# An H3 convolution and a linear-attention block on one core: 3,712 added matmuls in small array tiles, behind the denominators and at the end

## The chip, the cores and the metric

The kernel runs on one core of one Trainium2 chip. Its engines are TensorE (PE, with PEld for its weight loads), VectorE (DVE), ScalarE (ACT), GpSimd (POOL) and SyncE (SP, which issues the DMAs). The metric is the device time of one execution in microseconds (us).

## What is computed

Two independent blocks on sequences of S = 2048 rows and D = 576 columns in bf16, whose outputs stand side by side in a result of 1 x 2048 x 1152.

```
A:  k_shift = sum over t<4 of k shifted by t rows, times shift_k
    kv = k_shift * v
    y  = irfft(rfft(kv, 2S) * rfft(ssm_k, 2S))[:S] + kv * ssm_D     # a causal convolution
    a  = q * y
B:  q, k, v = x @ wqkv, 32 heads of 18
    phi(t) = where(t > 0, t + 1, exp(t)) + 1e-6
    kv = phi(k)^T v ;  z = sum over s of phi(k)
    b  = ((phi(q) kv) / (phi(q) z + 1e-6)) @ wo
result = concat(a, b)
```

## The kernel before

Block A is a long convolution written as matmuls with DFT matrices. The D = 576 channels are cut into five chunks (`ACH`: four of 128, one of 64). For each chunk the filter (`h`) and the input (`u`) go through the same stages. `h_T` transposes the filter on TensorE. `s1` (line 460) multiplies with the DFT matrix `K.G`, eight 128x128x128 matmuls for one PSUM tile. `tr` (line 467) is a DMA transpose of the evicted tile `Ch` or `Cu` into `Cth` or `Ctu`; these share two buffers. `s2` (line 483) does eight matmuls with 64 contraction rows, 32 output columns and 512 moving columns, in eight different array tiles. `prod` multiplies filter and input on DVE, `i1` (line 507) and `i2` (lines 520 and 521) transform back, and DVE multiplies by q. The shift convolution `conv` runs on DVE and POOL.

Block B makes `pqT` = phi(q) transposed (`b_q`, line 406) and `pk` = phi(k) (`b_k`, line 397). `b_G` (line 570) forms x^T phi(k), `b_kv` (583, 590) the per-head products and sums, and `b_M` (601) folds `wo` in. `b_den` makes the denominators: twenty matmuls of 512 columns (line 610) and twenty of one column (line 614), each with 32 output columns, go to four column tiles of `den_ps`; then DVE adds and takes the reciprocal `rden` (lines 617 to 621). `b_bc` (line 635) spreads `rden` over the heads and scales `pqT`, and `b_out` (line 644) multiplies with `M`, evicts on ACT (649) and stores by DMA (650).

The order of the work is written out by hand: `ORDER` is a string of units, such as `den`, `o.3` (rows 3 of `b_out`) or `h2.2.1.1.A` (stage `s2` of the filter, chunk 2, half 1, x = 1, evicted by ACT). Each unit issues its instructions to all engines as it is reached, and each engine runs its own instructions in that order. All matmul results go to one PSUM pool of four buffers, named `psum` (line 257), with the one tag `big`; each buffer is two banks of 512 float32. A unit that asks for a tile gets the buffer that was taken four requests before, and its first matmul waits until that one's readers are through.

Around the first place of the change the order is `i2.0.1 h2.2.0.0.A h2.2.1.0.A den h2.2.1.1.A i1.1.1.0.A lwo M.0 ... ut.2.0 u2.2.0.0.A M.2 ut.2.1 bc.3.0`. At the end it is `o.2 i2.4.0 st.2 o.8 o.10`. The kernel already has a unit that issues matmuls whose result is not read: `wu.40` (`_warm`, line 64), forty of 128x128 with 128 columns on a tile of zeros, near the start. `K.F[0]`, which the change reads, is one of the two transposed DFT matrices, 128 x 2048 in bf16, made by `f_T` near the start and read by `i2` until the end.

Of the kernel before, what the change touches and what calls it, by code (L numbers as in the profile page):

```python
# [8 lines left out]
FP32 = mybir.dt.float32  # L9
# [19 lines left out]

ORDER = """  # L30
wm io wu.0 ix.0 sin.1 id ix.1 hl.0 iw wk wu.40 sin.0 hT.0.D FT.1.D h1.0.0.0.A h1.0.1.0.A FT.0.D h1.0.1.1.A
h1.0.0.1.A iv sw W lw.0 xd.2 q.2.0 hc lw.1 k.8 q.2.2 q.2.1 ls Wj hl.1 hT.1.D k.9 k.11 k.10 h1.1.1.0.D xd.0 k.3
kl.0 cv.0.0.D one h1.1.0.0.A k.1 ht.0.0 h2.0.0.0.A h2.0.0.1.A eps cv.0.1.DD cv.0.2.DD q.0.1 h1.1.1.1.A q.0.0
h1.1.0.1.A xd.3 q.3.0 q.0.2 vl.0 cv.0.3.PDD k.2 cv.1.0.P k.0 ht.0.1 h2.0.1.1.A q.3.1 k.12 u1.0.1.1.A k.15
h2.0.1.0.D ht.1.1 h2.1.1.0.A k.13 u1.0.0.1.A hl.2 hT.2.D u1.0.0.0.A cv.1.1.PD k.14 xd.1 u1.0.1.0.A xl.2
cv.1.2.DD cv.1.3.DPP ht.1.0 xl.1 h2.1.1.1.A q.1.1 h2.1.0.1.A h2.1.0.0.A q.1.0 q.1.2 h1.2.1.0.A ut.0.1 k.7
u2.0.1.0.D u2.0.1.1.A k.6 h1.2.0.1.A k.4 ut.0.0 u2.0.0.1.D u2.0.0.0.A k.5 pX.0.0 pT.0.0 u1.1.1.0.A u1.1.1.1.A
q.3.2 u1.1.0.1.A xl.0 xl.3 kl.1 pX.0.1 pT.0.1 u1.1.0.0.A es G.0 vl.1 h1.2.0.0.A h1.2.1.1.A cv.2.0.D cv.2.1.DD
cv.2.2.DD G.2 ut.1.0 G.4 u2.1.0.1.D u2.1.0.0.A ut.1.1 i1.0.0.1.A hl.3 i1.0.0.0.A i1.0.1.1.A i1.0.1.0.A
cv.2.3.DDD ql.0 cv.3.0.D cv.3.1.DD u2.1.1.1.A ht.2.0 u2.1.1.0.A pX.1.1 pT.1.1 hT.3.A G.1 lwv pX.1.0 pT.1.0  # L40
h2.2.0.1.A ht.2.1 G.3 cv.3.2.DD u1.2.0.0.A i2.0.0 kl.2 u1.2.1.1.A u1.2.1.0.A kv u1.2.0.1.A i2.0.1 h2.2.0.0.A
h2.2.1.0.A den h2.2.1.1.A i1.1.1.0.A lwo M.0 i1.1.0.1.A i1.1.0.0.A i1.1.1.1.D ut.2.0 u2.2.0.0.A M.2 ut.2.1
bc.3.0 u2.2.0.1.A bc.0.1 h1.3.0.1.A bc.4.0 h1.3.0.0.A bc.0.0 h1.3.1.1.A vl.2 h1.3.1.0.A hl.4 ht.3.0 i2.1.1 M.1
u2.2.1.1.A cv.3.3.PPP bc.2.0 M.4 i2.1.0 cv.4.0.P M.3 u2.2.1.0.A bc.1.0 u1.3.0.0.A ht.3.1 hT.4.D u1.3.1.0.A
u1.3.1.1.D pX.2.1 u1.3.0.1.A cv.4.1.PP o.3 ql.1 pX.2.0 pT.2.0 pT.2.1 h2.3.0.1.A h2.3.0.0.A ut.3.0 o.0 o.7 bc.2.1
h2.3.1.1.A h2.3.1.0.A i1.2.0.0.D cv.4.2.PP cv.4.3.DDP i1.2.0.1.A i1.2.1.0.A i1.2.1.1.A ut.3.1 bc.1.1 bc.3.1 o.5
i2.2.0 u2.3.0.0.A u2.3.0.1.A i2.2.1 u1.4.1.1.A o.6 u1.4.1.0.D u1.4.0.0.A bc.4.1 u1.4.0.1.A ut.4.0 h1.4.1.1.A o.1
u2.3.1.0.D u2.3.1.1.A pX.3.1 h1.4.0.1.A o.11 h1.4.0.0.A h1.4.1.0.D ht.4.0 o.14 o.9 pT.3.1 pX.3.0 pT.3.0
u2.4.0.1.A u2.4.0.0.D ql.2 i1.3.1.0.A i1.3.1.1.A i1.3.0.1.D st.0 i1.3.0.0.A h2.4.0.0.D h2.4.0.1.A pX.4.0 o.15
i2.3.1 o.12 pT.4.0 i2.3.0 st.1 o.4 i1.4.0.1.D i1.4.0.0.A o.13 i2.4.1 o.2 i2.4.0 st.2 o.8 o.10  # L50
"""


# [12 lines left out]
def _warm(tc, psum, K, n):  # L66

    nc = tc.nc
    zero = K.sm[:, 1984:2048].bitcast(BF)
    if n:  # L70
        ps = psum.tile([128, 128], FP32, name="warm_ps", tag="big")
        for _ in range(n):
            nc.tensor.matmul(ps[:], lhsT=zero, rhs=zero, start=True, stop=True)
    else:
        nc.vector.memset(zero, 0.0)


def _head_consts(tc, cpool, K):
# [153 lines left out]
def kernel(  # L232
# [13 lines left out]
    nc = tc.nc  # L246
# [3 lines left out]
    q = A_q[0]  # L250
    k = A_k[0]
# [5 lines left out]
    psum = ctx.enter_context(tc.tile_pool(name="psum", bufs=4, space=PSUM))  # L257
# [33 lines left out]
    big = ctx.enter_context(tc.tile_pool(name="big", bufs=1, side="right"))  # L291
# [24 lines left out]
    K = Consts()  # L316
# [16 lines left out]
    Wj = lpool.tile([128, 4, D], BF, name="Wj")  # L333
# [42 lines left out]
    st = {}  # L376
# [24 lines left out]
    def b_q(g, pair):  # L401
        ps = psum.tile([128, 2, 512], FP32, name="q_ps", tag="big")
        for j, c in enumerate(pair):
            h0, hn = HCH[c]
            for t in range(5):
                nc.tensor.matmul(ps[0:hn, j, :], lhsT=wqk[:, t, h0:h0 + hn], rhs=xT[g][:, t, :],  # L406
                                 start=(t == 0), stop=(t == 4))
        n = len(pair)
        hn = HCH[pair[0]][1]
        phi(ps[0:hn, 0:n, :], pqT[0:hn, pair[0]:pair[0] + n, g * 512:(g + 1) * 512], hn)  # L410
# [253 lines left out]
    def pair(g, n):  # L664
        b_q(g, ((0, 1), (2, 3), (4,))[n])

    UNITS = {
        'xl': load_x, 'one': ones, 'wm': one_w, 'lw': load_w, 'ls': load_shift, 'Wj': shift_w, 'eps': eps_col,
        'id': lambda: _ident(tc, cpool, K), 'io': lambda: _small(tc, cpool, slotx, K),
# [16 lines left out]
        'pX': lambda ci, f: prod(ci, f, 'X'),  # L686
        'i1': i1, 'i2': i2, 'st': store_A,
        'k': b_k, 'q': pair, 'lwv': load_wv, 'lwo': load_wo, 'G': b_G, 'kv': b_kv, 'M': b_M,
        'den': b_den, 'es': b_esel, 'wu': lambda n: _warm(tc, psum, K, n), 'bc': b_bc, 'o': b_out,
    }  # L690
    with tc.manual_schedule():
        for unit in ORDER.split():
            name, *arg = unit.split('.')
            UNITS[name](*[int(c) if c.isdigit() else c for c in arg if c])

# [29 lines left out]
```

## Time and profile before

| | |
|---|---|
| median of 2 runs (170.94 to 171.16) | 171.05 us |
| span of the profiled execution | 170.0 us |
| the median less this span: what lies around it | 1.05 us |
| instructions | 4,984 |
| matmuls, and as many weight loads | 2,176 |
| DMA packets, bytes | 81,704, 32.58 MB |
| mean granted TensorE clock over the span | 0.995 |

The page gives the busy time of each engine, the chain of work that ended last, and the costliest groups of instructions. A row of a group names line, engine, operation, the tiles it writes and reads, the weights' rows*columns, the moving operand's shape and the count; then busy time in us, the mean of one in ns, and the idle time ahead with what ended it. In the timeline a row begins with start and length, in the chain too; in the view by stretches the columns are PE, PEld, DVE, ACT and POOL busy time with counts, then the granted clock, the DMA engines' share, and GB/s. A matmul's mean is from its start to its modelled end; consecutive ones overlap, so that their rate is higher than one by that mean.

### The profile page before, as it was taken

How to read it: one execution, taken by the hardware profiler on the slowest of the kernel's cores; microseconds unless marked ns; L12 is line 12 of the kernel's file. 1: busy time of each engine (PE TensorE's matmuls, PEld its weight loads, DVE VectorE, ACT ScalarE, POOL GpSimd, SP SyncE). 2: the span in 40 equal slices, each digit the busy share in tenths (PEclk: the TensorE clock that was granted, in tenths of full speed). 3: DMA queues.
4: the chain of work that ended last, by engine and by line, in shares of the span. 5: the costliest groups of instructions: out<-in, count | busy, mean ns of one | idle time of the engine just before them, and what ended most of it. 6: DMA issues, size and time to landing. Idle time of an engine off the chain costs nothing.

```text
span 170.0 us, 4984 instructions
## 1 busy us (share of the span) xinstructions
PE 159.0 (94%) x2176; PEld 106.9 (63%) x2176; DVE 139.7 (82%) x159; ACT 122.8 (72%) x142; POOL 70.9 (42%) x76
## 2 busy tenths in 40 slices
PE   4779999999999799999999999999999999999990
PEld 4768566665575456565685586857856765677750
DVE  7995589998989867999599887997999777999530
ACT  3458987977788899923597477989897778784431
POOL 7998982027693397000000049999900400000000
PEclk9999999999999999999999999999999999999997
DMA  5999699799989999999998655980959957988685
GB/s 147 273 268 250 119 267 136 137 272 225 145 183 217 263 178 318 290 213 219 306 214 196 106 150 40 182 159 18 146 126 276 202 128 69 237 180 258 191 244 117
DMA packets 81704, 32.58 MB, mean 192 GB/s; under 512 B 57432, under 2 KB 80978, under 8 KB 81682
## 3 DMA queue, kind: packets, MB, share of 16 engines
q1 hardware_dynamic: 81682, 32.26, 91.0%
q8 instruction: 17, 0.28, 0.7%
q14 instruction: 5, 0.04, 0.1%
HBM read 15.48 MB, written 4.72 MB: 119 GB/s over the span
## 4 chain that ended last, share of the span: by engine, by line
PE 77%; DMA 11%; DVE 6%; ACT 3%; issue 0%; ACTq 0%
PE q_ps L406 12%; PE g_ps L570 12%; PE k_ps L397 11%; PE o_ps L644 10%; PE s_ps L460 8%; PE i_ps L507 8%; DMA Ctu<-Cu 7%; PE s_ps L483 5%; DMA Cth<-Ch 4%; PE hT_ps L443 2%; PE i_ps L520 2%; PE i_ps L521 2%; PE bc_ps L635 1%; PE kv_ps L583 1%; DVE mp L138 1%; DVE mp L139 1%
## 5 line engine op out<-in xcount | busy, mean ns | idle before, releaser
L429 POOL TENSOR_TENSOR at<-k,Wj 128x2048 bf16<-128x2048 bf16 (+1 forms) x5 | 16.4, 3289 | 36.3 <-DVE at L430 36.2
L406 PE MATMUL q_ps<-xT,wqk 128*126 128x512 bf16 (+1 forms) x100 | 23.3, 381 | 0.0
L644 PE MATMUL o_ps<-wo_M,pqT 126*128 126x512 bf16 (+3 forms) x160 | 21.9, 286 | 0.0
L397 PE MATMUL k_ps<-wqk,xT 128*128 128x512 bf16 (+1 forms) x160 | 21.8, 286 | 0.0
L460 PEld LDWEIGHTS <-G 128*128 128x128 bf16 x320 | 17.6, 98 | 5.2 <-issue 2.1
L570 PE MATMUL g_ps<-pk,x_sb 128*128 128x512 bf16 (+3 forms) x160 | 20.4, 286 | 0.0
L277 ACT ACTIVATE Cu<-s_ps 128x1024 bf16<-128x1024 f32 (+1 forms) x18 | 16.6, 951 | 2.8 <-PE s_ps L460 2.4
L397 PEld LDWEIGHTS <-xT 128*128 128x128 bf16 x160 | 11.4, 98 | 11.1 <-issue 1.1
L644 PEld LDWEIGHTS <-pqT 126*128 126x128 bf16 (+1 forms) x160 | 11.2, 97 | 10.7 <-issue 0.8
L406 PEld LDWEIGHTS <-wqk 128*126 128x126 bf16 (+1 forms) x100 | 12.5, 131 | 8.2 <-issue 1.2
L277 ACT ACTIVATE Ch<-s_ps 128x1024 bf16<-128x1024 f32 (+1 forms) x18 | 16.3, 952 | 1.4 <-PE s_ps L460 0.8
L507 PE MATMUL i_ps<-W,T 64*128 64x128 bf16 x288 | 16.6, 216 | 0.4 <-DVE pqT L638 0.4
L649 ACT ACTIVATE ob<-o_ps 128x576 bf16<-128x576 f32 x16 | 10.4, 653 | 8.9 <-PE o_ps L644 8.7
L570 PEld LDWEIGHTS <-x_sb 128*128 128x128 bf16 (+1 forms) x160 | 10.8, 101 | 9.5 <-issue 0.2
L507 PE MATMUL i_ps<-W,X 64*128 64x128 bf16 x288 | 16.5, 216 | 0.0
L277 ACT ACTIVATE T<-s_ps 128x1024 bf16<-128x1024 f32 x16 | 15.8, 1021 | 0.6 <-PE s_ps L483 0.6
L277 ACT ACTIVATE V<-i_ps 128x1024 bf16<-128x1024 f32 x14 | 13.6, 1027 | 2.8 <-PE i_ps L507 2.1
L390 DVE SCALAR_TENSOR_TENSOR pqT<-pqT,q_ps 126x1024 bf16<-126x1024 bf16 (+1 forms) x12 | 12.2, 1037 | 3.8 <-ACT pqT L389 3.8
L522 DVE TENSOR_TENSOR q<-i_ps,q 128x1024 bf16<-128x1024 f32 (+1 forms) x10 | 11.2, 1116 | 4.6 <-PE i_ps L521 4.6
L389 ACT ACTIVATE pqT<-q_ps,neg 126x1024 bf16<-126x1024 f32 (+1 forms) x12 | 11.6, 968 | 4.3 <-PE q_ps L406 4.3
L430 POOL TENSOR_TENSOR at<-at 128x2048 bf16<-128x2048 bf16 (+1 forms) x4 | 12.4, 3094 | 5.4 <-DVE at L429 5.2
L433 POOL TENSOR_TENSOR v<-at,v 128x2048 bf16<-128x2048 bf16 (+1 forms) x3 | 10.3, 3419 | 9.8 <-DVE at L430 9.6
(120 smaller groups left out, 335.4 us busy)
## 6 DMA issues: line engine op xcount, KB each, us to landing
x_sb<-in_B_x_dram SPq DMA_DIRECT2D x4, 576.0 KB
out_dram<-ob SPq DMA_DIRECT2D x16, 144.0 KB, 4.0
h_sb<-in_A_ssm_k_dram SPq DMA_DIRECT2D x4, 512.0 KB
k<-in_A_k_dram SPq DMA_DIRECT2D x2, 1024.0 KB, 9.1
v<-in_A_v_dram SPq DMA_DIRECT2D x2, 1024.0 KB, 6.6
q<-in_A_q_dram SPq DMA_DIRECT2D x2, 1024.0 KB
out_dram<-q SPq DMA_DIRECT2D x2, 1024.0 KB
wqk<-in_B_wqkv_dram SPq DMA_DIRECT2D x2, 576.0 KB
```

The costliest lines, as they stand in the source:

```text
L277: nc.scalar.activation(out=out, in_=in_, func=ACT.Copy)
L389: nc.scalar.activation(out=out_ap, in_=ps_ap, func=ACT.Exp, bias=K.neg1[0:n, :])
L390: nc.vector.scalar_tensor_tensor(out=out_ap, in0=out_ap, scalar=1.0, in1=ps_ap, op0=ALU.min, op1=ALU.max)
L397: nc.tensor.matmul(ps[:, n0:n1], lhsT=xT[r // 4][:, t, rr * 128:(rr + 1) * 128], rhs=wqk[:, t, D + n0:D + n1], start=(t == 0), stop=(t == 4))
L406: nc.tensor.matmul(ps[0:hn, j, :], lhsT=wqk[:, t, h0:h0 + hn], rhs=xT[g][:, t, :], start=(t == 0), stop=(t == 4))
L429: on[0].tensor_tensor(out=t_, in0=kk[:, 3 - stage:19 - stage], in1=wb(stage), op=ALU.mult)
L430: on[1].tensor_tensor(out=a_, in0=a_, in1=t_, op=ALU.add)
L460: nc.tensor.matmul(ps[:, bi, 0:dc], lhsT=K.G[ri][:, b, :], rhs=xf(b), start=True, stop=True)
L507: nc.tensor.matmul(ps[:, r, g, :], lhsT=s[key, hf][64 * r:64 * r + 64, z, x, 128 * g:128 * g + 128], rhs=K.W[64 * r:64 * r + 64, m, :], st ...
L522: nc.vector.tensor_tensor(out=qs, in0=ps[:, :, 0:dc], in1=qs, op=ALU.mult)
L570: nc.tensor.matmul(ps[0:fn, n0:n1], lhsT=x_sb[:, r, f0:f0 + fn], rhs=pk[:, r, n0:n1], start=(r == 0), stop=(r == 15))
L644: nc.tensor.matmul(ps[:, n0:n1], lhsT=pqT[0:hn, c, r * 128:(r + 1) * 128], rhs=B['M'][0:hn, c, n0:n1], start=(c == 0), stop=(c == 4))
```

## The change

A function `_tiles` issues matmuls of given kinds, and a unit `pb` calls it: `pb.1` stands in `ORDER` right behind `den`, `pb.2` at the very end. Beside these two words the string is only broken into lines in another way. No unit is moved or removed, and nothing reads what the added matmuls write.

A kind is (kr, mc, n, count, step, mix): kr contraction rows, mc weight columns, n moving columns, `count` matmuls, each with its own weight load. They go round all 128/kr x 128/mc tiles of the array, the row tile changing fastest, and each row tile writes its own PSUM bank. The weights are columns of `K.F[0]`, shifted by one from matmul to matmul; with step 16 they are sixteen columns apart. With mix, one matmul of the full array with 512 columns follows every sixteen. `pb.1` has two kinds, 512 + 256 = 768 matmuls; `pb.2` has eleven, 2,944, with 32 more full ones from the mix.

```diff
+def _tiles(tc, psum, zero, kinds):
+    nc = tc.nc
+    for kind in kinds:
+        kr, mc, n, count, step, mix = kind
+        nr, ncol = 128 // kr, 128 // mc
+        ps = [psum.tile([128, 2, 512], FP32, name="tiles_ps", tag="big") for _ in range((nr + 1) // 2 + mix)]
+        for i in range(count):
+            r, c = i % nr, i // nr % ncol
+            rows = zero[kr * r:kr * r + kr]
+            nc.tensor.matmul(ps[r // 2][mc * c:mc * c + mc, r % 2, 0:n],
+                             lhsT=rows[:, i % 64:i % 64 + mc * step].rearrange("p (a s) -> p a s", s=step)[:, :, 0],
+                             rhs=rows[:, 0:n], start=True, stop=True)
+            if mix and i % 16 == 15:
+                nc.tensor.matmul(ps[-1][:, 0, :], lhsT=zero[:, 0:128], rhs=zero[:, 0:512], start=True, stop=True)
...
+    def tiles(part):
+        zero = K.F[0][:].rearrange("p b k -> p (b k)")
+        if part == 1:
+            _tiles(tc, psum, zero, ((64, 32, 64, 512, 1, 0), (64, 64, 64, 256, 1, 0)))
+        else:
+            _tiles(tc, psum, zero, ((64, 32, 64, 512, 1, 0), (64, 32, 64, 256, 16, 0), (64, 64, 64, 512, 1, 0),
+                                    (64, 64, 32, 256, 1, 0), (32, 64, 64, 256, 1, 0), (32, 32, 64, 256, 1, 0),
+                                    (128, 128, 128, 64, 1, 0), (128, 64, 64, 128, 1, 0), (128, 64, 128, 64, 1, 0),
+                                    (64, 64, 64, 512, 1, 1), (64, 128, 128, 128, 1, 0)))
...
-h2.2.1.0.A den h2.2.1.1.A i1.1.1.0.A lwo M.0 i1.1.0.1.A i1.1.0.0.A i1.1.1.1.D ut.2.0 u2.2.0.0.A M.2 ut.2.1
+u1.2.1.1.A u1.2.1.0.A kv u1.2.0.1.A i2.0.1 h2.2.0.0.A h2.2.1.0.A den pb.1 h2.2.1.1.A i1.1.1.0.A lwo M.0 i1.1.0.1.A
...
-i2.3.1 o.12 pT.4.0 i2.3.0 st.1 o.4 i1.4.0.1.D i1.4.0.0.A o.13 i2.4.1 o.2 i2.4.0 st.2 o.8 o.10
+o.2 i2.4.0 st.2 o.8 o.10 pb.2
...
-        'den': b_den, 'es': b_esel, 'wu': lambda n: _warm(tc, psum, K, n), 'bc': b_bc, 'o': b_out,
+        'den': b_den, 'es': b_esel, 'wu': lambda n: _warm(tc, psum, K, n), 'pb': tiles, 'bc': b_bc, 'o': b_out,
```

More of the change, by code (lines that the diff above doesn't have):

```diff
@@ L31 @@
 wm io wu.0 ix.0 sin.1 id ix.1 hl.0 iw wk wu.40 sin.0 hT.0.D FT.1.D h1.0.0.0.A h1.0.1.0.A FT.0.D h1.0.1.1.A
[L32 to L40, printed above, removed]
@@ L41 @@
-h2.2.0.1.A ht.2.1 G.3 cv.3.2.DD u1.2.0.0.A i2.0.0 kl.2 u1.2.1.1.A u1.2.1.0.A kv u1.2.0.1.A i2.0.1 h2.2.0.0.A
-h2.2.1.0.A den h2.2.1.1.A i1.1.1.0.A lwo M.0 i1.1.0.1.A i1.1.0.0.A i1.1.1.1.D ut.2.0 u2.2.0.0.A M.2 ut.2.1
-bc.3.0 u2.2.0.1.A bc.0.1 h1.3.0.1.A bc.4.0 h1.3.0.0.A bc.0.0 h1.3.1.1.A vl.2 h1.3.1.0.A hl.4 ht.3.0 i2.1.1 M.1
-u2.2.1.1.A cv.3.3.PPP bc.2.0 M.4 i2.1.0 cv.4.0.P M.3 u2.2.1.0.A bc.1.0 u1.3.0.0.A ht.3.1 hT.4.D u1.3.1.0.A
-u1.3.1.1.D pX.2.1 u1.3.0.1.A cv.4.1.PP o.3 ql.1 pX.2.0 pT.2.0 pT.2.1 h2.3.0.1.A h2.3.0.0.A ut.3.0 o.0 o.7 bc.2.1
@@ L46 @@
[L46 to L49, printed above, removed]
-i2.3.1 o.12 pT.4.0 i2.3.0 st.1 o.4 i1.4.0.1.D i1.4.0.0.A o.13 i2.4.1 o.2 i2.4.0 st.2 o.8 o.10
+h1.0.0.1.A iv sw W lw.0 xd.2 q.2.0 hc lw.1 k.8 q.2.2 q.2.1 ls Wj hl.1 hT.1.D k.9 k.11 k.10 h1.1.1.0.D xd.0 k.3 kl.0
@@ new lines @@
+cv.0.0.D one h1.1.0.0.A k.1 ht.0.0 h2.0.0.0.A h2.0.0.1.A eps cv.0.1.DD cv.0.2.DD q.0.1 h1.1.1.1.A q.0.0 h1.1.0.1.A
+xd.3 q.3.0 q.0.2 vl.0 cv.0.3.PDD k.2 cv.1.0.P k.0 ht.0.1 h2.0.1.1.A q.3.1 k.12 u1.0.1.1.A k.15 h2.0.1.0.D ht.1.1
+h2.1.1.0.A k.13 u1.0.0.1.A hl.2 hT.2.D u1.0.0.0.A cv.1.1.PD k.14 xd.1 u1.0.1.0.A xl.2 cv.1.2.DD cv.1.3.DPP ht.1.0
+xl.1 h2.1.1.1.A q.1.1 h2.1.0.1.A h2.1.0.0.A q.1.0 q.1.2 h1.2.1.0.A ut.0.1 k.7 u2.0.1.0.D u2.0.1.1.A k.6 h1.2.0.1.A
+k.4 ut.0.0 u2.0.0.1.D u2.0.0.0.A k.5 pX.0.0 pT.0.0 u1.1.1.0.A u1.1.1.1.A q.3.2 u1.1.0.1.A xl.0 xl.3 kl.1 pX.0.1
@@ new lines @@
+pT.0.1 u1.1.0.0.A es G.0 vl.1 h1.2.0.0.A h1.2.1.1.A cv.2.0.D cv.2.1.DD cv.2.2.DD G.2 ut.1.0 G.4 u2.1.0.1.D
+u2.1.0.0.A ut.1.1 i1.0.0.1.A hl.3 i1.0.0.0.A i1.0.1.1.A i1.0.1.0.A cv.2.3.DDD ql.0 cv.3.0.D cv.3.1.DD u2.1.1.1.A
+ht.2.0 u2.1.1.0.A pX.1.1 pT.1.1 hT.3.A G.1 lwv pX.1.0 pT.1.0 h2.2.0.1.A ht.2.1 G.3 cv.3.2.DD u1.2.0.0.A i2.0.0 kl.2
+u1.2.1.1.A u1.2.1.0.A kv u1.2.0.1.A i2.0.1 h2.2.0.0.A h2.2.1.0.A den pb.1 h2.2.1.1.A i1.1.1.0.A lwo M.0 i1.1.0.1.A
+i1.1.0.0.A i1.1.1.1.D ut.2.0 u2.2.0.0.A M.2 ut.2.1 bc.3.0 u2.2.0.1.A bc.0.1 h1.3.0.1.A bc.4.0 h1.3.0.0.A bc.0.0
@@ new lines @@
+h1.3.1.1.A vl.2 h1.3.1.0.A hl.4 ht.3.0 i2.1.1 M.1 u2.2.1.1.A cv.3.3.PPP bc.2.0 M.4 i2.1.0 cv.4.0.P M.3 u2.2.1.0.A
+bc.1.0 u1.3.0.0.A ht.3.1 hT.4.D u1.3.1.0.A u1.3.1.1.D pX.2.1 u1.3.0.1.A cv.4.1.PP o.3 ql.1 pX.2.0 pT.2.0 pT.2.1
+h2.3.0.1.A h2.3.0.0.A ut.3.0 o.0 o.7 bc.2.1 h2.3.1.1.A h2.3.1.0.A i1.2.0.0.D cv.4.2.PP cv.4.3.DDP i1.2.0.1.A
+i1.2.1.0.A i1.2.1.1.A ut.3.1 bc.1.1 bc.3.1 o.5 i2.2.0 u2.3.0.0.A u2.3.0.1.A i2.2.1 u1.4.1.1.A o.6 u1.4.1.0.D
+u1.4.0.0.A bc.4.1 u1.4.0.1.A ut.4.0 h1.4.1.1.A o.1 u2.3.1.0.D u2.3.1.1.A pX.3.1 h1.4.0.1.A o.11 h1.4.0.0.A
@@ L51 @@
+h1.4.1.0.D ht.4.0 o.14 o.9 pT.3.1 pX.3.0 pT.3.0 u2.4.0.1.A u2.4.0.0.D ql.2 i1.3.1.0.A i1.3.1.1.A i1.3.0.1.D st.0
+i1.3.0.0.A h2.4.0.0.D h2.4.0.1.A pX.4.0 o.15 i2.3.1 o.12 pT.4.0 i2.3.0 st.1 o.4 i1.4.0.1.D i1.4.0.0.A o.13 i2.4.1
+o.2 i2.4.0 st.2 o.8 o.10 pb.2
 """
```

## The prediction

> **What bounds the kernel now.** First the page's shares and its chain that ended last:
>
> ```profile
> PE 159.0 (94%) x2176; PEld 106.9 (63%) x2176; DVE 139.7 (82%) x159; ACT 122.8 (72%) x142; POOL 70.9 (42%) x76
> PE 77%; DMA 11%; DVE 6%; ACT 3%; issue 0%; ACTq 0%
> ```
>
> TensorE (PE) is busy for 94% of the span and carries 77% of the chain. What is put into its queue in the middle therefore moves nearly everything after it. Next the chain in order of time, at the two places of the change (start, length, what):
>
> ```profile
> 105.38 0.11 PE den_ps L614 x19
> 105.49 0.34 PE s_ps L483 x8
> 105.83 1.00 PE i_ps L507 x32
> ...
> 163.28 2.48 PE o_ps L644 x20
> 165.76 0.02 issue
> 165.78 0.65 ACT ob L649
> ```
>
> The first addition stands between 105.49 and the eight s_ps matmuls; there PE goes on without a gap. The second stands behind the last o_ps matmul at 165.76. The stretches around them:
>
> ```profile
> 106.00:112.00 6.00, 5.93 (x150) 4.54 (x145) 5.84 (x4) 5.71 (x7) 5.92 (x2) 1.00 0.89 168
> 112.00:120.00 8.00, 7.24 (x94) 5.17 (x92) 6.74 (x7) 7.10 (x10) 7.77 (x5) 1.00 0.45 91
> 165.80:170.00 4.20, 0.00 (x0) 0.00 (x0) 0.00 (x0) 0.64 (x1) 0.00 (x0) 0.79 0.52 117
> ```
>
> PE works 5.93 of 6 us behind the first place, and not at all in the last 4.2 us: only there is cover, 170.0 - 165.76 = 4.24 us, while the last eviction and output DMA finish.
>
> **What a small matmul costs.** A row's mean is a latency; the rate is read from how many fit into a time. From the groups by shape, the timeline and the chain:
>
> ```profile
> L483 PE MATMUL s_ps<-Cth,W 64*32 64x512 bf16 x144 | 6.1, 383 | 0.9 <-DMA Cth<-Ch 0.9
> 105.42 0.41 PE L483 MATMUL s_ps<-Cth,W 64*32 64x512 bf16 x8
> 83.09 0.56 PE s_ps L483 x16
> 83.65 3.68 PE i_ps L507 x128
> 14.52 0.89 PE s_ps L460 x16
> 101.85 0.36 PE z_ps L590 x5
> ```
>
> Eight 64x32 matmuls in eight different tiles end 0.41 us after the first began, though one takes 0.383: seven steps in 0.027 us, 3.9 ns each, weight load included. I call such a set a round. Sixteen take 0.56 us on the chain and eight 0.34, so one more round of 512 columns is 0.22 us, and 0.12 us of the 0.34 is the change to another tile form. At 128 columns a full-array matmul steps by 0.89/16 = 56 ns, and i_ps L507, in two 64-row tiles, by 3.68/64 = 57.5 ns per round of two. With one column, den_ps L614 takes 0.11 us for nearly five rounds of four: 25 ns. The line through 220 and 56 ns gives 29 ns for a round of 64 columns; for 32 columns I take the 25.
>
> The other half is supply: can instructions arrive at one pair (weight load and matmul) every 3.6 ns for longer than one burst? The page shows how the program is loaded:
>
> ```profile
> q8 instruction: 17, 0.28, 0.7%
> ```
>
> 2,176 + 2,176 PE instructions in 17 packets is 256 each: 128 pairs a packet. 0.7% of 16 engines' 170.0 us is 19.0 us, 1.12 us a packet, or 8.75 ns a pair if one packet follows another. Bounds of the supply: 3.9 ns (the burst above, 16 instructions long) and 28.75 ns (i_ps L507: 128 pairs in 3.68 us, the fastest stretch as long as a packet). I take 8.75, nearest to the row that measures the loading itself, with one packet already there at the start (the L507 stretch uses up a packet without a gap).
>
> **Part 1, 768 pairs behind the denominators.** By the array: 512 in eight tiles are 64 rounds, 64 x 29 = 1.86 us; 256 in four tiles of 64x64 are 64 rounds, 1.86 us; two more changes of form, 0.24: 3.96 us. By the supply: 128 pairs at 3.6 ns (0.46) and 640 at 8.75 (5.60), with 0.24: 6.30 us, which I take. At 28.75 ns it is 22.3.
>
> Nothing covers it: the rows show PE without a gap there. DVE's reciprocal runs beside it and will end earlier relative to PE, but PE has other work before the first bc_ps anyway. The later PE idles, 0.42 and 0.31 us, might be filled:
>
> ```profile
> 114.80 0.61 PE L460 MATMUL s_ps<-hT,G 128*128 128x128 bf16 x8 [0.42 <-ACT Ch L277]
> 115.71 0.61 PE L460 MATMUL s_ps<-hT,G 128*128 128x128 bf16 x8 [0.31 <-ACT Ch L277]
> 107.48 6.13 DMA Ctu<-Cu
> 104.02 6.10 SPq L467 DMA_TRANSPOSE Ctu<-Cu  x2
> ```
>
> They hang on the landing of Ctu. The second transpose (ut.2.1) reuses the buffer that h2.2.1.1 reads, which is the unit right behind the added matmuls. So SP's queue waits longer too (its v and h loads behind it as well), and I let this idle move along: gain 0, at best 0.73. The two PSUM buffers that part 1 takes were last read by i2.0.1 (DVE) and h2.2.0.0 (ACT). A late reader there would cost at most one eviction, 1.02 us; I take 0:
>
> ```profile
> 103.60 1.23 DVE L522 TENSOR_TENSOR q<-i_ps,q 128x1024 bf16<-128x1024 f32 x1 [0.35 <-PE i_ps L521]
> 103.97 2.95 ACT L277 ACTIVATE T<-s_ps 128x1024 bf16<-128x1024 f32 x3 [0.24 <-PE s_ps L483]
> ```
>
> DVE is through at 104.83 and ACT's first of three before 105.49.
>
> **Part 2, 2,944 pairs and 32 full ones at the end.** By the array, in the order of the code: 512 in 64x32 1.86; 256 of the same with weights 16 columns apart 0.93; 512 in 64x64 (128 rounds) 3.71; 256 in 64x64 of 32 columns (64 rounds at 24 to 25 ns) 1.54; 256 in 32x64 0.93; 256 in 32x32, 3.3 to 3.9 ns each, 0.85. These 2,048 pairs make 9.82 us. Then 64 full ones at 56 ns 3.56; 128 in 128x64 1.86; 64 in 128x64 of 128 columns 1.79; 128 in 64x128 as in L507 3.68. The mixed kind: sixteen small ones are four rounds and a change of form (0.23 us), and a lone 512-column matmul between two forms is 0.34 less the burst, 0.32; 32 x 0.55 = 17.6. Ten changes of form at 0.12 are 1.2. Sum by the array: 39.5 us.
>
> Unknown prices: weights of 64 columns. The five L590 matmuls load up to 126 columns for 7 moving ones, 72 ns each, so 64 columns are at most 36 ns against 29; under the supply rate a round of four takes 35 anyway: 0. Spaced weights: transposing h_sb loads its columns 16 apart too (sixteen in 1.15 us below), 72 ns against 56, so at most 0.5 us over 32 rounds; these have a quarter of the columns, and I take 0.
>
> ```profile
> 87.88 1.15 PE hT_ps L443 x16
> ```
>
> By the supply the first 2,048 take 0.46 + 1,920 x 8.75 ns (16.8) = 17.3 us in place of 9.8; the kinds behind them need a pair only every 14 ns or more, and stay. 17.3 + 28.5 + 1.2 = 47.0. At 28.75 ns it is 90.4. The 4.24 us behind 165.76 now lie beside this; closing after the last matmul I estimate at 0.3 (its latency is 0.2 to 0.4 in the rows): net 47.0 - 3.94 = 43.1.
>
> **Sum.** The profiled execution has a span of 170.0 us; the median of the runs is 171.05, so 1.05 lies around it and stays. 171.05 + 6.3 + 43.1 = 220.4 us.
>
> The Trainium skill's page "Runtime: NRT & Kernel Launch", section "Instruction fetch mechanics", says that PE holds 2,048 instructions, refilled in blocks of 256, and that crossing a block is mostly hidden. The trace agrees on the block (256 a packet); how many are held no run here shows. By that rule the sum is the array's, the first rival.
>
> **The rivals.** Array alone: if several packets are loaded ahead, 1,536 instructions of part 1 are all there, and the refill at 1.12 us a packet keeps up with part 2. For it: L507 used up a packet, and PE stood still for none. Against: nothing in the trace ever drew more than 256 instructions in 3.68 us. 171.05 + 3.96 + 39.5 - 3.94 = 210.6 us.
>
> Loading without overlap: if a packet is only asked for when the last one is begun, and the asking takes as long as the transfer, 2.24 us for 128 pairs, 17.5 ns each. Part 1 11.9, part 2 34.1 + 28.9 + 1.2 = 64.1: 243.1 us. At the bound of 28.75 ns, 279.8.
>
> A halved clock: PE can run slower than the granted-clock column says.
>
> ```profile
> L73 PE MATMUL warm_ps<-sm 128*128 128x128 bf16 x40 | 4.4, 313 | 2.4 <-DVE sm L75 2.4
> ```
>
> These 40 at the start take 110 ns each, twice the 56 of later ones. If many small tiles count as little activity, rounds double: 7.9 and 79 us, 254 us. Against: no row in the middle shows it. The page "TensorE: Matmul & The Clock Gate" of the Trainium skill, Part 1, describes such a gate, half rate until the array has been busy; the L73 row agrees, and whether small tiles count as busy no row shows.
>
> Not slower: matmuls whose result nobody reads might be dropped when the kernel is built; then the time stays 171. L73 speaks against it: 40 such matmuls are in the trace. Hiding cannot do it: at 3.9 ns a pair 2,976 pairs are 11.6 us, and only 4.24 + 3.4 (2%) are free at the end; it would decide from 2.6 ns.
>
> **How the numbers follow.** Forecast 0.42, array alone 0.25, loading without overlap 0.18, halved clock 0.10, bound of the supply 0.03, not slower 0.02. The likeliest gives 220.4. From 206 (array alone, less 0.73 and some of the mixed kind) to 250 lie the first three, 0.85; the halved clock is left out. A measurement of this kernel tells about 2% from no change: faster 0.01, same 0.01, slower 0.98.
>
> **What would show it.** In the profile after: some 29 more instruction packets on q8 (7,488 instructions); about 6 us of small matmuls behind L614, and the eight s_ps that much later; in part 2 the 64x32 kind in 4 to 5 us (1.9 for the array alone, 9 without overlap), and each mixed group of 17 in 0.55 us. The 128x128 kind at 56 ns shows the clock. I am wrong if the first kinds step by rounds of 29 ns, or stop at every 128 pairs for over a microsecond.

## The result, and the profile after

The changed kernel takes 281.45 us (280.45 to 282.45, 2 runs) against 171.05: 1.645 times as long, 95% interval 1.630 to 1.659. The forecast was 220.4 us with a range to 250. That it gets much slower was right; the size was not. Where two runs of one kernel lie over 1.5% apart, the longer one at a lower clock, only the shorter is used; of the experiments this concerns `lumps192`. From `_tiles` on the line numbers of the kernel after are 17 higher: L500 is the L483 of before, L524 the L507, and L88 and L92 are the added matmuls. The page of the kernel after, its shares, its code packets and the costliest group:

```profile
PE 226.2 (81%) x5920; PEld 162.0 (58%) x5920; DVE 139.6 (50%) x159; ACT 122.8 (44%) x142; POOL 70.8 (25%) x76
PEclk9989999999999999555999999997555555559999
...
q8 instruction: 46, 0.75, 1.2%
...
PE 73%; issue 17%; DVE 4%; DMA 3%; ACT 1%; SPq 1%; ACTq 0%
...
L88 PE MATMUL tiles_ps<-F 64*32 64x64 bf16 (+8 forms) x3712 | 58.2, 224 | 46.3 <-issue 46.3
```

In 110 more microseconds PE is busy for only 67 more. The added matmuls stood idle for 46.3 us with nothing in the trace to wait for ("issue"), and that cause has 17% of the chain where it had 0%. There are 29 more packets of instructions, as forecast; 1.2% of 16 engines' 280.7 us is 53.9 us, 1.17 us each. The clock column shows half speed in two places. The timeline of PE through part 1 (start, length, what, idle before it):

```profile
106.42 1.11 PE L88 MATMUL tiles_ps<-F 64*32 64x64 bf16 x115
109.13 1.21 PE L88 MATMUL tiles_ps<-F 64*32 64x64 bf16 x128 [1.60 <-issue]
112.86 1.27 PE L88 MATMUL tiles_ps<-F 64*32 64x64 bf16 x128 [2.52 <-issue]
116.86 1.28 PE L88 MATMUL tiles_ps<-F 64*32 64x64 bf16 x128 [2.73 <-issue]
120.59 1.99 PE L88 MATMUL tiles_ps<-F 64*32 64x64 bf16 x128 [2.45 <-issue]
124.32 1.92 PE L88 MATMUL tiles_ps<-F 64*64 64x64 bf16 x128 [1.74 <-issue]
128.04 0.38 PE L88 MATMUL tiles_ps<-F 64*64 64x64 bf16 x13 [1.81 <-issue]
128.35 0.63 PE L500 MATMUL s_ps<-Cth,W 64*32 64x512 bf16 x8
```

Between the first and the last, each piece is 128 pairs, that is 256 instructions, exactly one packet; then PE stands still. From one start to the next it is 3.73, 4.00, 3.73, 3.73 and 3.72 us. The pieces at 120.59 and 124.32 are slower (1.9 in place of 1.2 us) and the gaps behind them shorter by as much: the period belongs to the packet and not to the matmuls. Part 1 lasts 128.35 - 106.42 = 21.9 us. The stretches of the whole (columns as before):

```profile
106.40:128.30 21.90, 9.05 (x784) 8.19 (x768) 4.27 (x3) 0.51 (x1) 17.48 (x7) 0.62 0.21 27
128.30:131.00 2.70, 2.70 (x53) 2.01 (x42) 0.00 (x0) 1.12 (x2) 0.00 (x0) 0.50 0.46 54
189.40:246.80 57.40, 24.57 (x2013) 22.49 (x2014) 0.00 (x0) 0.65 (x1) 0.00 (x0) 0.54 0.06 13
246.80:252.60 5.80, 5.77 (x93) 5.68 (x93) 0.00 (x0) 0.00 (x0) 0.00 (x0) 0.58 0.01 3
252.60:257.70 5.10, 4.55 (x201) 4.27 (x198) 0.00 (x0) 0.00 (x0) 0.00 (x0) 1.00 0.01 3
257.70:276.10 18.40, 18.40 (x550) 9.83 (x548) 0.00 (x0) 0.00 (x0) 0.00 (x0) 1.00 0.02 4
276.10:280.70 4.60, 3.72 (x129) 3.55 (x128) 0.00 (x0) 0.00 (x0) 0.00 (x0) 1.00 0.02 4
```

Part 2's first six kinds but for their last 35 pairs (189.4 to 246.8) take 57.4 us, with PE busy for 24.6 of them. The DMA engines move almost nothing else there (a share of 0.06), so other transfers don't set the period. The later kinds need a packet less often and run without long gaps.

### The profile page after: what moved, and what is told of

It reads as the page before. It is cut to its first block, busy times and chain, and to the rows that moved or that the text cites. A ratio compares the mean times of both kernels' runs of the same rounds, so it can differ in the third digit from the quotient of the medians.

```text
span 280.7 us, 12473 instructions
## 1 busy us (share of the span) xinstructions
PE 226.2 (81%) x5920; PEld 162.0 (58%) x5920; DVE 139.6 (50%) x159; ACT 122.8 (44%) x142; POOL 70.8 (25%) x76
## 4 chain that ended last, share of the span: by engine, by line
PE 73%; issue 17%; DVE 4%; DMA 3%; ACT 1%; SPq 1%; ACTq 0%
PE tiles_ps L88 20%; PE o_ps L661 7%; PE q_ps L423 7%; PE g_ps L587 7%; PE k_ps L414 6%; PE s_ps L477 6%; PE i_ps L524 5%; PE tiles_ps L92 4%; PE s_ps L500 4%; DMA Cth<-Ch 3%; PE i_ps L537 2%; PE i_ps L538 1%; PE bc_ps L652 1%; PE hT_ps L460 1%; PE kv_ps L600 1%
## 5 line engine op out<-in xcount | busy, mean ns | idle before, releaser
L88 PE MATMUL tiles_ps<-F 64*32 64x64 bf16 (+8 forms) x3712 | 58.2, 224 | 46.3 <-issue 46.3
L88 PEld LDWEIGHTS <-F 64*64 64x64 bf16 (+6 forms) x3712 | 51.0, 120 | 56.9 <-issue 56.2
L294 ACT ACTIVATE T<-s_ps 128x1024 bf16<-128x1024 f32 x16 | 15.8, 1021 | 22.6 <-PE s_ps L500 22.6
L661 PE MATMUL o_ps<-wo_M,pqT 126*128 126x512 bf16 (+3 forms) x160 | 21.9, 286 | 0.0
L477 PEld LDWEIGHTS <-G 128*128 128x128 bf16 x320 | 18.4, 100 | 5.6 <-ACT G L229 2.8
L524 PE MATMUL i_ps<-W,T 64*128 64x128 bf16 x288 | 17.6, 224 | 0.4 <-DVE pqT L655 0.4
L524 PE MATMUL i_ps<-W,X 64*128 64x128 bf16 x288 | 17.5, 224 | 0.0
L296 DVE CAST V<-i_ps 128x1024 bf16<-128x1024 f32 x4 | 4.9, 1224 | 24.4 <-DMA Drow<-in_A_ssm_D_dram 23.7
L477 PE MATMUL s_ps<-hT,G 128*128 128x128 bf16 (+1 forms) x160 | 11.6, 223 | 2.8 <-ACT G L229 2.7
```

Of the source, the lines that this page charges most:

```text
L88: nc.tensor.matmul(ps[r // 2][mc * c:mc * c + mc, r % 2, 0:n], lhsT=rows[:, i % 64:i % 64 + mc * step].rearrange("p (a s) -> p a s", s=ste ...
L294: nc.scalar.activation(out=out, in_=in_, func=ACT.Copy)
L477: nc.tensor.matmul(ps[:, bi, 0:dc], lhsT=K.G[ri][:, b, :], rhs=xf(b), start=True, stop=True)
L524: nc.tensor.matmul(ps[:, r, g, :], lhsT=s[key, hf][64 * r:64 * r + 64, z, x, 128 * g:128 * g + 128], rhs=K.W[64 * r:64 * r + 64, m, :], st ...
L661: nc.tensor.matmul(ps[:, n0:n1], lhsT=pqT[0:hn, c, r * 128:(r + 1) * 128], rhs=B['M'][0:hn, c, n0:n1], start=(c == 0), stop=(c == 4))
```

## The experiments

Three theories were set against each other. **Loading**: one packet of 256 instructions is on order ahead, a new one is to be had only every 3.73 us or so, and whoever eats faster waits. **Issue**: PE's sequencer needs 28 to 29 ns for each pair of small tiles, wherever it stands. **Clock**: the halved clock slows the array, and that sets the time. Each run came with runs of the kernel before on the same chip; that kernel took 171.4 us beside the first four experiments and 172.7 beside the other five.

**Each part alone.** `p1_alone` leaves `pb.2` out of `ORDER`, `p2_alone` leaves `pb.1` out.

```diff
-o.2 i2.4.0 st.2 o.8 o.10 pb.2
+o.2 i2.4.0 st.2 o.8 o.10
```

> Only the 768 matmuls behind the denominators. Loading theory (a packet of 256 instructions every 3.73 us, one on order ahead): they take 21.9 us as in the kernel after, the work behind them loses another 1.7 us at the halved clock, and the time is 171.05 + 23.6 = 194.7 us. Issue theory (every pair of small tiles costs 28 to 29 ns in PE's own sequencer): 21.9 us too, with PE never idle for microseconds. If the parts cost something only together, it is less than 190.

> Only the matmuls at the end. Loading theory: 90.3 us behind the last o_ps matmul as in the kernel after, less the 4.24 us that were there, and about 0.8 of closing: 171.05 + 86.9 = 257.9 us. The sum of both parts alone is then the whole: 23.6 + 86.9 = 110.5 against the measured 110.4. A remainder of over 2 us would mean that part 1 changes what part 2 costs.

Measured 195.0 us (1.139, 1.125 to 1.153) and 258.6 us (1.511, 1.500 to 1.522). Over the 171.4 beside them that is 23.6 and 87.2, together 110.8, against the 110.4 of the kernel after. The parts simply add; neither explains the other.

**The same instructions with more columns.** `wide` changes only the moving columns of the starved kinds.

```diff
-((64, 32, 64, 512, 1, 0), (64, 64, 64, 256, 1, 0))
+((64, 32, 384, 512, 1, 0), (64, 64, 192, 256, 1, 0))
...
-((64, 32, 64, 512, 1, 0), (64, 32, 64, 256, 16, 0), (64, 64, 64, 512, 1, 0),
- (64, 64, 32, 256, 1, 0), (32, 64, 64, 256, 1, 0), (32, 32, 64, 256, 1, 0),
+((64, 32, 384, 512, 1, 0), (64, 32, 384, 256, 16, 0), (64, 64, 192, 512, 1, 0),
+ (64, 64, 192, 256, 1, 0), (32, 64, 384, 256, 1, 0), (32, 32, 384, 256, 1, 0),
```

> The same instructions, but the two kinds of part 1 and the first six of part 2 stream up to six times the columns (384 in place of 64 in tiles of 32 weight columns, 192 in place of 64 or 32 in tiles of 64). By the array that is 13 to 21 ns a pair at full clock. Loading theory: still 3.73 us per 128 pairs, so part 1 takes 21 to 22 us and the first six kinds 56 to 60; the gaps shrink to about 1 us, PE is busy enough to keep the full clock, and the whole is 275 to 281 us. Clock theory (the halved array sets the time): six times the columns take several times as long, part 1 over 60 us and the whole over 400. Issue theory: as loading, but without gaps.

Measured 276.4 us (1.614, 1.603 to 1.626). Three to six times the columns, and the time is 5 us less. Timeline and stretches of `wide`, part 1 and the first six kinds of part 2:

```profile
112.28 2.80 PE L88 MATMUL tiles_ps<-F 64*32 64x384 bf16 x128 [0.66 <-issue]
116.01 2.79 PE L88 MATMUL tiles_ps<-F 64*32 64x384 bf16 x128 [0.93 <-issue]
119.74 3.02 PE L88 MATMUL tiles_ps<-F 64*32 64x384 bf16 x128 [0.93 <-issue]
```

```profile
106.10:127.30 21.20, 17.24 (x780) 13.29 (x768) 4.28 (x3) 0.49 (x1) 17.52 (x7) 1.00 0.23 27
186.80:243.60 56.80, 43.67 (x2053) 36.20 (x2049) 0.00 (x0) 0.65 (x1) 0.00 (x0) 1.00 0.06 13
```

Again 128 pairs every 3.73 us, with 2.8 us of work in place of 1.2, and 21.2 and 56.8 us in all. The clock theory falls: at full clock the same time passes. PE busy for 81% (17.24 of 21.2) kept the clock at 1.00; 41% (9.05 of 21.9) in the kernel after did not. So the halved clock is a consequence of the gaps, and it costs what `wide` saves, about 5 us.

The two runs also show when a packet is asked for. Between 112 and 122 us the DMA engines move nothing but packets of instructions; each of the forty figures is a slice of 0.25 us, and a packet is counted in the slice in which its transfer begins. First the kernel after, then `wide`:

```profile
GB/s 0 0 0 0 0 0 0 0 66 0 0 0 0 0 0 0 0 0 0 0 0 0 0 66 0 0 0 0 0 0 0 0 0 0 0 0 0 0 66 0
q8 instruction: 3, 0.05, 2.4%
...
GB/s 0 0 0 0 0 66 0 0 0 0 0 0 0 0 0 0 0 0 0 0 66 0 0 0 0 0 0 0 0 0 0 0 0 0 0 0 66 0 0 0
q8 instruction: 3, 0.05, 2.2%
```

In the kernel after the transfers begin in the slices from 114.00, 117.75 and 121.50, in `wide` in those from 113.25, 117.00 and 121.00. That is 0.9 to 1.5 us behind the start of a piece in both (112.86, 116.86 and 120.59; 112.28, 116.01 and 119.74), although a piece of 64x32 tiles lasts 1.3 us in the one and 2.8 in the other: the transfer follows the start of a piece and not its end. It takes 1.2 to 1.3 us (2.4% and 2.2% of 16 engines' 10 us, for three packets), and from its landing some 1.4 us, the rest of the 3.73, pass until PE begins on the new packet. So in these stretches each packet is asked for only when PE has begun on the one before it, and about 1.1, 1.2 and 1.4 us follow one another; what the first and the last of them consist of, no row shows.

**The same columns in an eighth of the instructions.** `few` has an eighth of the count and eight times the columns in the same kinds.

```diff
-((64, 32, 64, 512, 1, 0), (64, 64, 64, 256, 1, 0))
+((64, 32, 512, 64, 1, 0), (64, 64, 512, 32, 1, 0))
...
-((64, 32, 64, 512, 1, 0), (64, 32, 64, 256, 16, 0), (64, 64, 64, 512, 1, 0),
- (64, 64, 32, 256, 1, 0), (32, 64, 64, 256, 1, 0), (32, 32, 64, 256, 1, 0),
+((64, 32, 512, 64, 1, 0), (64, 32, 512, 32, 16, 0), (64, 64, 512, 64, 1, 0),
+ (64, 64, 256, 32, 1, 0), (32, 64, 512, 32, 1, 0), (32, 32, 512, 32, 1, 0),
```

> The same streamed columns in an eighth of the instructions: in part 1 and the first six kinds of part 2 a count of an eighth with eight times the columns (512, or 256 where there were 32). Loading theory: part 1 is 192 instructions and takes about 3.8 us by the array (16 rounds of 0.22 and changes of form), the six kinds of part 2 about 10; the other kinds about 31. The whole is 171.05 + 3.8 + 41 - 3.5 = 212 us, that is, the array's sum of the prediction (210.6). Clock theory: the rounds run at half rate, part 1 near 7.5 and the whole near 240. Issue theory: 212 as well.

Measured 211.1 us (1.233, 1.222 to 1.244). Part 1 of `few`:

```profile
104.49 3.77 PE L88 MATMUL tiles_ps<-F 64*32 64x512 bf16 x96
108.19 0.41 PE L500 MATMUL s_ps<-Cth,W 64*32 64x512 bf16 x8
```

3.7 us without a gap, where the forecast's array sum had 3.96. The whole is within 0.5 us of the array's sum in the prediction, 210.6: for rounds of 512 and 256 columns the prices of rounds and changes of form hold, and with an eighth of the instructions the supply costs nothing that shows. Rounds of 64 columns in small tiles, which the forecast put at 29 ns, this run doesn't test.

**The same instructions in other places.** `spread48` puts 48 matmuls behind each of the sixteen k units, `lumps192` 192 behind four of them; both leave the two places of the change empty.

```diff
-            _tiles(tc, psum, zero, ((64, 32, 64, 512, 1, 0), (64, 64, 64, 256, 1, 0)))
+            _tiles(tc, psum, zero, ((64, 32, 64, 48, 1, 0),))
```

> 768 matmuls of 64x32 with 64 columns again, but 48 behind each of the sixteen k units (wide matmuls that use up only some 16 instructions a microsecond) in place of one lump behind the denominators, and none at the end. Loading theory: the packets are there in time, each lump costs what PE needs to take 48 pairs (8.3 ns each, 0.4 us) and two changes of form (0.24), 16 x 0.64 = 10 us; the whole is 179 to 184 us, the clock stays full, and no gap of microseconds appears. Issue theory (28 to 29 ns a pair wherever it stands): 1.35 us a lump and 0.24, 25 us, so 194 to 197.

> The same 768 matmuls in four lumps of 192 pairs (384 instructions, one and a half packets), behind k.8, k.1, k.13 and k.5, none at the end. Loading theory with one packet on order ahead: what is left of the packet in use and the next whole one are there, 128 to 256 pairs; so each lump takes 1.6 us for its pairs and none or one gap of up to 2.5 us, 1.8 to 4.3 us a lump, the whole 178 to 188 us. A deeper stock would show no gap at all and 178. Issue theory: 5.5 us a lump without a gap, 193 or more.

`spread48` measured 186.5 us (1.081, 1.063 to 1.100), 13.8 over its neighbour. One of the fifteen lumps without a gap, and the only one with a gap inside:

```profile
20.36 0.55 PE L88 MATMUL tiles_ps<-F 64*32 64x64 bf16 x48
...
75.20 0.26 PE L88 MATMUL tiles_ps<-F 64*32 64x64 bf16 x17
77.17 0.31 PE L88 MATMUL tiles_ps<-F 64*32 64x64 bf16 x31 [1.71 <-issue]
```

A lump takes 0.49 us from its start to the next unit (20.36 to 20.85), 10 ns a pair: the issue theory, with 28 a pair anywhere, falls. The total is above my 179 to 184, and one gap of 1.71 us appeared where I expected none. The lumps make 7.8, issue gaps in tiles_ps and s_ps 2.5; PE waited 1.3 us in q_ps for DVE, and in s_ps for ACT's tile G 2.6 in place of 1.2. That is 13.0 of the 13.8; the rest I have not assigned.

`lumps192` took 188.97 us, 16.3 over its neighbour and 1 us above the expected 178 to 188; the other of its two runs took 193.21. Its four lumps:

```profile
18.75 0.83 PE L88 MATMUL tiles_ps<-F 64*32 64x64 bf16 x82
20.03 1.22 PE L88 MATMUL tiles_ps<-F 64*32 64x64 bf16 x110 [0.45 <-issue]
33.05 1.88 PE L88 MATMUL tiles_ps<-F 64*32 64x64 bf16 x177
37.47 0.25 PE L88 MATMUL tiles_ps<-F 64*32 64x64 bf16 x15 [2.55 <-issue]
58.24 1.75 PE L88 MATMUL tiles_ps<-F 64*32 64x64 bf16 x192
80.51 1.87 PE L88 MATMUL tiles_ps<-F 64*32 64x64 bf16 x192
```

After 82 or 177 pairs the stock was empty; two lumps got through whole. That is the rest of one packet and at most one more. But then the units behind paid, which I had not priced:

```profile
PE hT_ps L460 <- issue: 3.3, 2, 3.0
PE tiles_ps L88 <- issue: 3.0, 2, 2.5
...
PE s_ps L477 <- issue: 1.8, 1, 1.8
```

5.1 of 8.1 us of gaps stand in hT_ps and s_ps, matmuls that nobody touched.

**One tile in place of many.** `onetile` is part 1 alone with 768 full matmuls of 64 columns.

```diff
-((64, 32, 64, 512, 1, 0), (64, 64, 64, 256, 1, 0))
+((128, 128, 64, 768, 1, 0),)
```

> Part 1 alone, its 768 matmuls as full 128x128 ones with 64 columns in place of small tiles. By the array they take 29 ns each, one behind another, 22.3 us. Loading theory: the same 256 instructions per 3.73 us are just enough, so the stretch takes 22 to 23 us, as long as the small tiles took; PE hardly idles, the clock stays full, and the 1.7 us behind it are saved: 192.5 to 194.5 us against 194.7 for small tiles. If small tiles themselves are what is slow, this is clearly faster, under 188.

Measured 193.8 us (1.123, 1.105 to 1.142). The group in `onetile`:

```profile
L88 PE MATMUL tiles_ps<-F 128*128 128x64 bf16 x768 | 22.6, 193 | 0.0
```

768 full matmuls, each with four or eight times the work of a small one, take 22.6 us without a gap, where the small ones took 21.9. In a stream this long the small tiles' concurrency buys nothing. At 29 ns each these matmuls run at the array's own price, which is also a packet's 128 pairs in 3.73 us, so that this run doesn't tell the two limits apart. The saving behind the stretch is too small for these runs: from the eight s_ps to the last eviction `onetile` needs 60.3 us (128.72 to 188.98) and `p1_alone` 61.7 (126.66 to 188.39).

**Smaller counts.** `p1_384` and `p1_96` are part 1 alone with a half and an eighth of the count; the diff is that of `p1_384`, `p1_96` has 64 and 32.

```diff
-((64, 32, 64, 512, 1, 0), (64, 64, 64, 256, 1, 0))
+((64, 32, 64, 256, 1, 0), (64, 64, 64, 128, 1, 0))
```

> Part 1 alone with half its count, 256 and 128 matmuls, none at the end. Loading theory: the first 115 pairs come from what is there, each further 128 pairs wait for a packet (3.73 us): 10.5 to 11.5 us for the stretch, and up to 1 us behind it at a lower clock; the whole is 182 to 184 us. A cost in proportion to the count would be half of part 1's 23.6: 183 as well.

> Part 1 alone with an eighth of its count, 64 and 32 matmuls (192 instructions, less than a packet), none at the end. Loading theory: the stretch itself takes 1.0 to 1.2 us without a gap, since 115 pairs were there before the first gap of the kernel after; but the packet is then used up, and the gap of 1.5 to 2.5 us falls on the units right behind (s_ps and i_ps, whose stream takes 256 instructions in 3.7 us by itself). The whole is 173.5 to 175.5 us. Cost in proportion to the count: 3.0 us, 174; issue theory: 2.8 us inside the stretch.

Measured 184.3 us (1.068, 1.050 to 1.086) and 175.0 us (1.014, 1.0003 to 1.028; the two runs leave open whether that is 2%). `p1_384` shows pieces of 115, 128, 128 and 13 in 10.6 us (106.12 to 116.76), as expected. In `p1_96` the stretch and the first gap behind it:

```profile
104.53 1.07 PE L88 MATMUL tiles_ps<-F 64*32 64x64 bf16 x96
105.53 0.41 PE L500 MATMUL s_ps<-Cth,W 64*32 64x512 bf16 x8
...
106.89 0.21 PE L524 MATMUL i_ps<-W,T 64*128 64x128 bf16 x1 [0.51 <-issue]
```

96 pairs go through in 1.0 us, 10 ns each, and the gap falls on i_ps behind them. It is 0.5 us and not the 1.5 to 2.5 I expected: the s_ps and i_ps in between (105.53 to 106.38) had covered 0.85 us of the packet's way.

## Why the prediction was wrong, point by point

- **Where it hurts: right.** Part 1 found no cover, part 2 only the last 4.24 us. Nothing else took or gave a large share: 21.9 (part 1) + 0.7 (the work behind it, 189.4 - 128.35 against 165.76 - 105.42) + 90.4 (part 2, 189.4 to the end of its matmuls at 279.8) + 0.9 (closing) - 4.24 = 109.7 of 110.4. The rest is within how far the start of part 1 and the time around the span moved between the two profiled runs (106.42 against 105.4; 0.75 against 1.05).
- **Prices by the array: right for long rounds, too low for small tiles of 64 columns.** `few`, with rounds of 512 and 256 columns, came out at 211.1 for 210.6. The mixed groups, forecast at 0.55 us, step by 18.4/32 = 0.575. Weights 16 columns apart and those of 64 columns cost nothing that shows beside the waiting. But the 3.6 ns a pair for code that is already there came from a burst of eight: a whole packet of 64x32 pairs took 1.21 us, 9.4 ns a pair. By that rate part 1 would take about 7 us with all its code at hand (an estimate, 768 x 9.4 ns), so that array alone, 210.6, was out of reach for this kernel, and the forecast's 6.3 would then have lain near the time by luck.
- **The supply: wrong, and this is the step that failed.** The prediction says "I take 8.75, nearest to the row that measures the loading itself", one packet behind another. A packet's transfer does take 1.17 us, but packets don't follow each other: a packet every 3.73 us, 29 ns a pair, is the upper bound that the prediction kept from L507 (28.75). It gave 279.8 for that bound, at a chance of 0.03, and left it out of the range. Part 1 is 21.9 in place of 6.3, the six kinds 57.4 in place of 17.3: 55.7 of the 61 us that were missing. Of the others, 3.3 stand in part 2's later kinds (33.0 us from 246.8 to 279.8 against 28.5 + 1.2). The prediction's own sign of being wrong, a stop at every 128 pairs for over a microsecond, came as it was written.
- **The rival that named the mechanism**, loading without overlap, had the right cause and a wrong price: I let the asking take as long as the transfer (2.24 us a packet). What lies around the transfer takes twice as long as the transfer itself, about 1.1 us before it and 1.4 behind it. That the packet is asked for when the last one is begun, the starts of the transfers in the kernel after and in `wide` show.
- **Why the row misled.** L507's 128 pairs in 3.68 us without a gap looked like a stream with room to spare. It runs at almost exactly the speed at which packets come. A stretch that doesn't wait shows a lower bound of the supply and nothing above it, and I spread the chance as if the middle were known.
- **The Trainium skill's page** "Runtime: NRT & Kernel Launch", section "Instruction fetch mechanics": the block of 256 agrees with the pieces of 128 pairs between two gaps. That PE holds 2,048 instructions, with crossings mostly hidden, does not: part 1 has 1,536 and stopped after 115 pairs, 230 instructions. The measurement decides.
- **The halved clock** came, as one rival had it, but as a consequence. While PE starves it hides in the gaps. It shows in the kinds that follow: 64 full matmuls of part 2 in 5.8 us in place of 3.56, at a clock of 0.58.

## What to carry to other kernels

Count instructions as well as array time: on PE a weight load and a matmul are two, and a stretch that asks for more than 256 instructions in 3.7 us runs at the speed of the program's loading once the one or two packets at hand are used up, whatever its tiles could do. The remedy is fewer, longer instructions (`few`), or small ones between long ones (`spread48`), in lumps well below a packet; and the gap may then appear in the units behind. An upper bound that nothing in the trace excludes belongs into the range.

## What the runs showed of the hardware

- Inside a packet PE takes small pairs at about 8 to 10 ns each (96 in 1.0 us, 128 in 1.2 us), far slower than the first burst of eight at 3.9 and far faster than the loading. The prediction had the array take 64x32 tiles at 3.6, an estimate. It isn't the array's clock that sets the 8 to 10: at half clock such a piece took 1.28 us (116.86), at full clock 1.21 (109.13). What sets it stays open.
- In the kernel after, PE's clock halved while PE worked 1.2 us of every 3.7; the full clock was gone 5 us into part 1:

```profile
106.00:110.00 4.00, 2.40 (x253) 2.15 (x246) 3.25 (x3) 0.91 (x1) 3.92 (x2) 1.00 1.10 137
110.00:115.00 5.00, 1.61 (x169) 1.38 (x157) 1.02 (x1) 0.00 (x0) 4.92 (x2) 0.67 0.03 7
115.00:120.00 5.00, 1.28 (x128) 1.15 (x128) 0.00 (x0) 0.00 (x0) 4.84 (x4) 0.50 0.02 3
130.00:135.00 5.00, 5.00 (x123) 4.09 (x120) 0.32 (x1) 3.58 (x5) 0.00 (x0) 0.78 1.03 167
```

No single gap there is longer than 2.73 us. The Trainium skill's page "TensorE: Matmul & The Clock Gate" (section "Why this matters for your kernels") warns of idle gaps of more than about 3 us; here shorter ones, repeated, were enough. From 128.35 on PE worked without a pause, and in the stretch from 130 the mean of 0.78 puts the return near 132.2 (2.2 us at half, 2.8 at full), about 4 us later.
